# Transposes and sums of logarithms as two 64-row products, and a low-rank product spread over four column groups

## The chip, the core and the metric

The kernel runs on one core of one Trainium2 chip. A core has five engines that work side by side: TensorE (PE in the profile) for matrix products and transposes, with its weight loads shown apart (PEld); VectorE (DVE) and ScalarE (ACT) for elementwise work and for taking results out of PSUM; GpSimd (POOL); and SyncE (SP), whose queue issues the DMAs here. The metric is the device time of one execution in microseconds (us). A profile shows one execution; the span of its instructions is a little shorter than its time.

## The reference

Two blocks in a row. The first is a gated linear attention, a recurrence over 768 tokens for each of 4 batches and 8 heads of 48 channels; its output, with heads side by side, is the input of the second, a token mixer of rank 32 followed by a channel network of 384, 1536 and 384 channels.

```python
def _attn_ref(q, k, v, f_logit):            # (4, 8, 768, 48)
    f = 1.0 / (1.0 + np.exp(-f_logit))
    for t in range(S):
        state = f[:, :, t, :, None] * state + np.einsum('bhd,bhe->bhde', k[:, :, t], v[:, :, t])
        y[:, :, t] = np.einsum('bhd,bhde->bhe', q[:, :, t], state)

def _moe_ref(x, U, V, w_ch1, w_ch2):        # x: (4, 768, 384), U: (768, 32), V: (32, 768)
    h = x.transpose(0, 2, 1) @ U @ V
    u = x + h.transpose(0, 2, 1)
    return u + np.maximum(u @ w_ch1, 0.0) @ w_ch2
```

All data is float32 (the weights U, V, w_ch1 and w_ch2 arrive as float64 and are turned into float32 on the chip).

## The kernel before

**Attention.** The 768 tokens of a batch are cut into 6 blocks of 128 (NBL), each of two chunks of 64 (C). A unit is one batch and two heads, 96 channels padded to 128 partitions, so there are 16 units, four to a batch. Within a chunk the recurrence becomes matrix products, after q and k have been multiplied by running products of the gates. For that q, k and the gates are needed with channels on partitions and time along the row, while they arrive with time on partitions. How they are turned differs by unit:

- Units 0 to 3 (batch 0): `on_tensor` (L723) turns k and q with six TensorE transposes of 128x128 each, and VectorE multiplies the result straight out of PSUM (`operand`, L737). The running products of the gates come from sums of logarithms: `log_sums` (L764) multiplies each block of logarithms (128 tokens by 128 channels) by the constant matrix `later`, 128 x 130, which holds a 64x64 triangle for each chunk and, in two more columns, the sum over a whole chunk. `keep_logs` (L777 to L782) exponentiates the sums on ScalarE.
- Units 4 and 5: f, k and q through `on_tensor`, then a sigmoid on ScalarE (L788) and scans on VectorE.
- Units 6 to 15: turned by VectorE's own transpose (L700). TensorE isn't used for it.

A unit then goes through `kept` (L924, transposes of k by halves: 64 partitions to 128x64, two at a time), `scores` (L897), `states` (L945), a scan over chunks (L967), `read` (L984) and `inner` (L1002).

**Mixer.** One for each batch, on x with tokens on partitions, six blocks of 128 tokens by 384 channels. `low_rank` (L182) multiplies each token block by its 128x32 piece of U. An output of 32 rows uses 32 columns of the array, so four token blocks run beside each other in four column groups; blocks 4 and 5 follow in groups 0 and 1. `added_up` (L190) adds the four groups up with the constant matrix `blocks`, and `mix` (L207) multiplies by V. `turn` (L255) transposes the mixed x of two token blocks with six transposes of 128x128 into PSUM and ScalarE copies them to uT (L256); `ch1` (L267) and `ch2` (L327) or their versions with fewer products (L356, L454) are the channel network. Mixer 0 has finer pieces: `low_rank_of` (L218), `added_up_of` (L227), `mix_of` (L243), `turn_of` (L279, copy L281), `ch1_of` (L293); `low_rank_of` runs on 288 channels first and on 96 later, when the last unit of the batch is done.

**Order.** The order on TensorE is written out by hand over the whole kernel: the mixer of one batch runs between the pieces of the next batch's attention. VectorE, ScalarE and the DMA queue also have a written order in batch 0; later ScalarE and VectorE are ordered by the program's order with priorities. In batch 0 the chain of one unit on TensorE is: `log_sums` of the next unit (L764), scores (L897), k transposes of the next unit (L723), read (L984), q transposes of the next unit (L723), kept (L924), inner (L1002), states (L945), then `log_sums` of the unit after that, which waits for ScalarE's logarithms (L757, L758), which wait for VectorE's floor (L755), which stands behind the multiplication of q (L737) in VectorE's order.

**PSUM.** Wide results (two banks) take turns in three buffers (`ps_big`), narrow ones in two (`ps_mm`).

A matrix product in float32 stands in the profile as two records, a transpose as one.

Of the kernel before, what the change touches and what calls it, by code (L numbers as in the profile page):

```python
# [156 lines left out]
class Mixer:  # L157
# [6 lines left out]
    def __init__(self, tc, b, x, U, V, w1, w2, sums, ident, blocks, out, two, three, zp, ps_big, ps_mm, wide=False,  # L164
# [11 lines left out]

        def low_rank():
            pm = ps_mm.tile([P, 512], F32, name="ph", tag="mm")

            for c in range(NCH):  # L180
                g = slice((c % NG) * R, (c % NG + 1) * R)
                nc.tensor.matmul(pm[g, 0:DM], lhsT=U[:, c, :], rhs=x[:, c, :],  # L182
                                 start=(c < NG), stop=(c >= NCH - NG))
            h[0] = two.tile([P, DM], F32, name="h", bufs=2)
            nc.scalar.copy(h[0], pm[:, 0:DM])
# [28 lines left out]
        def low_rank_of(cols):  # L214
            pm = ps_mm.tile([P, 512], F32, name="ph", tag="mm")
            for c in range(NCH):
                g = slice((c % NG) * R, (c % NG + 1) * R)
                nc.tensor.matmul(pm[g, cols], lhsT=U[:, c, :], rhs=x[:, c, cols],  # L218
                                 start=(c < NG), stop=(c >= NCH - NG))
# [29 lines left out]
        def turn(a):  # L249
# [3 lines left out]
            for s in range(2):  # L253
                for m in range(NDC):
                    nc.tensor.transpose(pt[:, s, m * P : (m + 1) * P], x[:, 2 * a + s, m * P : (m + 1) * P], ident)  # L255
            nc.scalar.copy(  # L256
                uT[a].rearrange("p m (s t) -> p s m t", s=2),
                pt[:, :, 0 : NDC * P].rearrange("p s (m t) -> p s m t", t=P),
# [12 lines left out]
        def turn_of(a, ms):  # L271
# [4 lines left out]
            pt = last["put"]  # L276
            for m in ms:
                for s in range(2):
                    nc.tensor.transpose(pt[:, s, m * P : (m + 1) * P], x[:, 2 * a + s, m * P : (m + 1) * P], ident)  # L279
            g = slice(ms[0], ms[-1] + 1)  # L280
            nc.scalar.copy(  # L281
                uT[a][:, g].rearrange("p m (s t) -> p s m t", s=2),
                pt[:, :, ms[0] * P : (ms[-1] + 1) * P].rearrange("p s (m t) -> p s m t", t=P),
            )
# [232 lines left out]
def factored_path(ctx, tc, q, k, v, f_logit, moe_U, moe_V, moe_w_ch1, moe_w_ch2, out, ok):  # L517
# [108 lines left out]
    later = const.tile([P, P + 2], F32, name="later")  # L626
    nc.vector.memset(later, 0.0)
    for s in range(2):
        half = later[s * C : (s + 1) * C, s * C : (s + 1) * C]
        nc.vector.memset(half, 1.0)  # L630
        nc.vector.memset(later[s * C : (s + 1) * C, P + s : P + s + 1], 1.0)
# [74 lines left out]
    def prepare(n):  # L706
# [12 lines left out]
        def on_tensor(nm):  # L719

            pt = ps_big.tile([P, 2, 512], F32, name="pt", tag="big")
            for c in range(NBL):
                nc.tensor.transpose(  # L723
                    pt[:, 2 * c // NBL, c % (NBL // 2) * P : (c % (NBL // 2) + 1) * P],
                    nat[n % 2][nm][:, c].rearrange("p h d -> p (h d)"), ident,
                )
            return pt[:, :, 0 : G * C].rearrange("p a (c t) -> p a c t", t=C)

        def halves(t):
            return t[:, 0:S].rearrange("p (a c t) -> p a c t", a=2, t=C)  # L730

        def operand(nm, of):
            t = T[nm] = kz[n % 2][:, C:] if nm == "k" else two.tile([P, S], F32, name="qT")
            if n < HP:
                pt = on_tensor(nm).rearrange("p a c t -> p a (c t)").rearrange("p a (c t) -> p t a c", c=NBL // 2)
                by_time = "p (t a c) -> p t a c"
                nc.vector.tensor_tensor(t.rearrange(by_time, a=2, c=NBL // 2), pt,  # L737
                                        T[of].rearrange(by_time, a=2, c=NBL // 2), ALU.mult)
# [21 lines left out]
        def log_sums():  # L760
            pt = T["sums"] = ps_big.tile([P, 2, 512], F32, name="pt", tag="big")
            for c in range(NBL):
                o = c % (NBL // 2) * (P + 2)
                nc.tensor.matmul(  # L764
                    pt[:, 2 * c // NBL, o : o + P + 2],
                    lhsT=nat[n % 2]["f"][:, c].rearrange("p h d -> p (h d)"), rhs=later, start=True, stop=True,
                )
# [813 lines left out]
```

## Time and profile before

| | us |
|---|---|
| median of 3 runs | 477.74 (477.48 to 478.96) |
| the profiled execution | 477.89 |
| its span | 476.2 |
| granted TensorE clock over the span | 0.998 |

| Group (records) | busy us | shape |
|---|---|---|
| transposes L723 (84) | 11.6 | 128 rows to 128x128 |
| transposes L255 and L279 (72) | 9.2 | 128 rows to 128x128 |
| sums of logarithms L764 (48) | 6.6 | 128 rows, 128x130 |
| low rank L182 and L218 (60) | 6.2 | 128 rows, 32 columns of the array |
| half transposes L924 (192) | 9.4 | 64 rows to 128x64 |
| channel network L267, L293, L327, L356, L454 | 380 | 128 rows |

The busy time of a group is the time in which at least one of its records runs. Records overlap, so the mean length of a record (272 ns for a transpose) is longer than its step to the next (109 ns in a row of transposes). What a group costs TensorE is therefore read from start to start in the timeline, not from the lengths. TensorE is busy for most of every fortieth of the span; the table says how little of that the changed groups make up, about 34 us of 460.

### The profile page before, as it was taken

Reading aid. Unit: us, or ns where it says so; the run is one execution under the profiler, and the core shown is the slowest. Engines: PE = TensorE matmul, PEld = TensorE weight load, DVE = VectorE, ACT = ScalarE, POOL = GpSimd, SP = SyncE. Lnnn points to the kernel's source line nnn. Section 1 sums busy time; section 2 is a strip of 40 time slices with the busy share of each in tenths; the row PEclk is TensorE's granted clock in tenths of the full one; section 3 lists DMA queues with packets and bytes.
Section 4 is the critical chain, followed back from the end, with each engine's and each line's share of the span. In section 5 each row is a group of like instructions: output and inputs, shape, how many; then the busy total and the mean of one; then the engine's idle time right before and its main releaser. Section 6 shows DMA issues by size and latency. Waiting matters only on the chain.

```text
span 476.2 us, 12778 instructions
## 1 busy us (share of the span) xinstructions
PE 459.8 (97%) x5547; PEld 397.5 (83%) x5547; DVE 349.0 (73%) x579; ACT 179.1 (38%) x327; POOL 36.1 (8%) x48
## 2 busy tenths in 40 slices
PE   7998999999999899999999999999999999999995
PEld 5886888875665478798898888999979999999994
DVE  5768789789999485677766538987796887858632
ACT  5775876663443133414242423451411311212200
POOL 2002345441000000000000000000000000000000
PEclk9999999999999999999999999999999999999999
DMA  9948987577777322155416100100000000000001
GB/s 193 192 117 199 218 201 187 128 137 110 115 116 129 59 43 34 24 70 99 60 36 100 27 33 3 28 3 21 17 1 1 34 1 31 5 4 30 2 34 39
DMA packets 148312, 34.35 MB, mean 72 GB/s; under 512 B 136790, under 2 KB 146710, under 8 KB 148246
## 3 DMA queue, kind: packets, MB, share of 16 engines
q1 hardware_dynamic: 148246, 33.44, 35.6%
q8 instruction: 45, 0.74, 0.7%
q14 instruction: 21, 0.17, 0.1%
HBM read 28.70 MB, written 4.72 MB: 70 GB/s over the span
## 4 chain that ended last, share of the span: by engine, by line
PE 75%; DVE 13%; DMA 3%; issue 3%; ACT 3%; SPq 2%; POOL 0%; DVEq 0%
PE pw L356 26%; PE pz L267 22%; PE pp L454 12%; PE sc L897 2%; DVE late L819 2%; PE po L327 2%; PE y L984 2%; PE put L255 2%; PE y L1002 1%; DVE added L967 1%; PE pt L924 1%; DVE late L801 1%; PE pu L207 1%; PE pt L764 1%; SPq L600 1%
## 5 line engine op out<-in xcount | busy, mean ns | idle before, releaser
L267 PE MATMUL pz<-uT,w 128*128 128x256 f32 x492 | 111.4, 382 | 1.1 <-ACT z_all L310 1.1
L267 PEld LDWEIGHTS pz<-uT,w 128*128 128x128 f32 x492 | 91.7, 190 | 14.0 <-ACT z_all L310 1.5
L356 PE MATMUL pw<-w,z_all 128*128 128x192 f32 x216 | 37.7, 329 | 0.0
L356 PE MATMUL pw<-zw,w_raw 128*128 128x192 f32 x216 | 37.3, 327 | 0.0
L356 PEld LDWEIGHTS pw<-zw,w_raw 128*128 128x128 f32 x216 | 35.2, 190 | 0.7 <-DVE w_raw L197 0.6
L356 PEld LDWEIGHTS pw<-w,z_all 128*128 128x128 f32 x216 | 35.0, 190 | 0.7
L310 ACT ACTIVATE z_all<-pz 128x512 f32<-128x512 f32 x33 | 19.7, 598 | 41.8 <-PE pz L267 41.6
L101 POOL TENSOR_TENSOR w<-w_y,w_r 128x384 int32<-128x384 int32 x24 | 31.5, 1311 | 38.8 <-DVE w_y L100 23.5
L972 ACT COPY st<-added 128x576 f32<-128x576 f32 x12 | 14.7, 1223 | 39.0 <-DVE added L967 39.0
L454 PE MATMUL pp<-v_nat,late 128*128 128x128 f32 x224 | 28.8, 275 | 0.0
L454 PEld LDWEIGHTS pp<-v_nat,late 128*128 128x128 f32 x224 | 27.0, 192 | 0.0
L327 PE MATMUL po<-w,z_all 128*128 128x384 f32 x72 | 24.9, 493 | 1.6 <-DVE o L197 1.6
L447 ACT ACTIVATE other<-other 128x512 f32<-128x512 f32 x18 | 11.3, 631 | 39.9 <-DVE other L197 39.9
L327 PE MATMUL po<-w,zw 128*128 128x384 f32 x72 | 25.3, 496 | 0.1
L910 DVE TENSOR_TENSOR A<-sc,causal 128x768 f32<-128x768 f32 x16 | 15.2, 951 | 12.2 <-PE sc L897 11.9
L801 DVE TENSOR_TENSOR_SCAN late<-fz,late 128x768 f32<-128x768 f32 x12 | 21.1, 1755 | 4.0 <-ACT fz L796 3.6
L327 PEld LDWEIGHTS po<-w,z_all 128*128 128x128 f32 x72 | 13.3, 190 | 10.5 <-DVE o L197 2.3
L327 PEld LDWEIGHTS po<-w,zw 128*128 128x128 f32 x72 | 13.1, 190 | 9.8 <-issue 1.2
L819 DVE TENSOR_TENSOR_SCAN late<-fz,other 128x768 f32<-128x768 f32 x12 | 21.0, 1747 | 0.2
L447 ACT ACTIVATE z_all<-z_all 128x512 f32<-128x512 f32 x12 | 7.6, 630 | 32.8 <-DVE z_all L197 32.8
L984 PEld LDWEIGHTS y<-st,qT 48*64 48x64 f32 x704 | 13.5, 137 | 7.1 <-issue 4.5
L952 ACT COPY added<-ds 48x576 f32<-48x576 f32 (+1 forms) x28 | 17.8, 636 | 3.9 <-PE ds L945 3.7
(223 smaller groups left out, 848.1 us busy)
## 6 DMA issues: line engine op xcount, KB each, us to landing
w_raw<-in_moe_w_ch_dram SPq DMA_DIRECT2D x18, 384.0 KB, 3.5
out_dram<-o SPq DMA_DIRECT2D x24, 192.0 KB, 1.9
v_nat<-in_v_dram SPq DMA_DIRECT2D x16, 144.0 KB, 3.7
v_nat<-in_v_dram SPq DMA_DIRECT2D x32, 72.0 KB, 3.7
zw<-in_moe_w_ch_dram SPq DMA_DIRECT2D x6, 384.0 KB, 4.9
w<-in_k_dram SPq DMA_DIRECT2D x4, 288.0 KB, 5.0
w<-in_q_dram SPq DMA_DIRECT2D x4, 288.0 KB, 5.6
late<-in_f_logit_dram SPq DMA_DIRECT2D x10, 96.0 KB, 2.8
```

The lines of the kernel that those rows point to most:

```text
L101: nc.gpsimd.tensor_tensor(dst.bitcast(I32), shaped(y.bitcast(I32)), shaped(r), ALU.add)
L267: nc.tensor.matmul(pm[:, i * 2 * P : (i + 1) * 2 * P], lhsT=w1[:, m, o : o + P], rhs=uT[a][:, m, :], start=(m == 0), stop=(m == NDC - 1))
L310: nc.scalar.activation(z[a, c][:, k : k + 2, :].rearrange("p i t -> p (i t)"), pm, AF.Relu)
L327: nc.tensor.matmul(pm, lhsT=z[a, i // NI][:, i % NI, s * P : (s + 1) * P], rhs=w2[:, i, :], start=(i == 0), stop=(i == NFC - 1))
L356: nc.tensor.matmul(pm[:, n * HM : (n + 1) * HM], lhsT=lhs[:, i, :], rhs=rhs[:, i, :], start=(i == 0), stop=(i == NI - 1))
L447: nc.scalar.activation(dst, dst, AF.Relu, scale=float(SIGNS[n]))
L454: nc.tensor.matmul(pm[:, i, r * P : (r + 1) * P], lhsT=room["w"](wn)[:, r * P : (r + 1) * P], rhs=x_node(a, xn), start=((xn, wn) == of[0]) ...
L801: nc.vector.tensor_tensor_scan(backwards(X, S - 1, S), backwards(f, S, S), backwards(ends, S - 1, S), 0.0, ALU.mult, ALU.add,)
L819: nc.vector.tensor_tensor_scan(Y, f[:, 0:S], starts, 0.0, ALU.mult, ALU.add)
L910: nc.vector.tensor_tensor(T["A"], sc[:, :, 0 : NBL * C].rearrange("p h (c i) -> p h c i", i=C), causal.unsqueeze(1).unsqueeze(1).broadcast ...
L952: nc.scalar.copy(added[r, 1:].rearrange("p (e c s) -> p e c s", c=NBL, s=2), ds[r, :, 0 : NBL * D].rearrange("p s (c e) -> p e c s", e=D),)
L984: nc.tensor.matmul(o(c % 2, par, c // 2), lhsT=T["q"][rows[par], chunk[c]], rhs=T["st"][rows[par], c, :], start=(c <= 2), stop=False, skip ...
```

## The change

Four groups of TensorE products are cut in another way. What is computed stays the same.

- `on_tensor`: each 128x128 transpose becomes two transposes of 64 partitions (a chunk) by 128 columns, which use the upper and the lower half of the array's rows. Chunk s of every block goes to PSUM bank s. VectorE and ScalarE read with patterns changed to suit (L737, L740, L788, L789).
- `turn` and `turn_of`: the same, through a new helper `turn_blocks`, with the two halves in two banks and the copy to uT by runs of 64 instead of 128.
- `log_sums`: each product of 128 rows by 130 columns becomes two of 64 rows by 65 columns, also in the two halves of the rows. `later` shrinks to 128 x 65 and needs one fill instead of five.
- `low_rank` and `low_rank_of`: a new helper `products_with_u`. Token blocks 0 to 3 go to the four column groups as before. Blocks 4 and 5 are cut in two halves of the channels, and the four halves go to the four groups. `added_up` adds the groups up anyway.

On TensorE the order of the groups is unchanged. On the DMA queue one weight load of batch 1 (a piece of w_ch2) moves behind one load of q; on GpSimd the building of the identity matrix moves one step.

```diff
+        def products_with_u(pm, cols):
+            left = NCH - NG
+            n = (cols.stop - cols.start) * left // NG
+            todo = [(c, c, cols) for c in range(NG)]
+            todo += [(i % left + NG, i, slice(cols.start + i // left * n, cols.start + (i // left + 1) * n)) for i in range(NG)]
+            for c, i, of in todo:
+                nc.tensor.matmul(pm[i * R : (i + 1) * R, of], lhsT=U[:, c, :], rhs=x[:, c, of],
+                                 start=(c < NG), stop=True, skip_group_check=True)
...
-            for c in range(NCH):
-                g = slice((c % NG) * R, (c % NG + 1) * R)
-                nc.tensor.matmul(pm[g, 0:DM], lhsT=U[:, c, :], rhs=x[:, c, :],
-                                 start=(c < NG), stop=(c >= NCH - NG))
+            products_with_u(pm, slice(0, DM))
...
-            for s in range(2):
-                for m in range(NDC):
-                    nc.tensor.transpose(pt[:, s, m * P : (m + 1) * P], x[:, 2 * a + s, m * P : (m + 1) * P], ident)
+            turn_blocks(a, range(NDC), pt)
+
+        def turn_blocks(a, ms, pt):
+            H = P // 2
+            for m in ms:
+                for s in range(2):
+                    for r in range(2):
+                        g = slice(r * H, (r + 1) * H)
+                        o = (2 * m + s) * H
+                        nc.tensor.transpose(pt[:, r, o : o + H], x[g, 2 * a + s, m * P : (m + 1) * P], ident[g, g])
             nc.scalar.copy(
-                uT[a].rearrange("p m (s t) -> p s m t", s=2),
-                pt[:, :, 0 : NDC * P].rearrange("p s (m t) -> p s m t", t=P),
+                uT[a][:, ms[0] : ms[-1] + 1].rearrange("p m (s r t) -> p r (m s) t", s=2, r=2),
+                pt[:, :, 2 * ms[0] * H : 2 * (ms[-1] + 1) * H].rearrange("p r (n t) -> p r n t", t=H),
             )
...
-    later = const.tile([P, P + 2], F32, name="later")
-    nc.vector.memset(later, 0.0)
+    later = const.tile([P, C + 1], F32, name="later")
+    nc.vector.memset(later, 1.0)
...
             for c in range(NBL):
-                nc.tensor.transpose(
-                    pt[:, 2 * c // NBL, c % (NBL // 2) * P : (c % (NBL // 2) + 1) * P],
-                    nat[n % 2][nm][:, c].rearrange("p h d -> p (h d)"), ident,
-                )
+                for s in range(2):
+                    g = slice(s * C, (s + 1) * C)
+                    nc.tensor.transpose(
+                        pt[:, s, c * C : (c + 1) * C], nat[n % 2][nm][g, c].rearrange("p h d -> p (h d)"), ident[g, g],
+                    )
...
             for c in range(NBL):
-                o = c % (NBL // 2) * (P + 2)
-                nc.tensor.matmul(
-                    pt[:, 2 * c // NBL, o : o + P + 2],
-                    lhsT=nat[n % 2]["f"][:, c].rearrange("p h d -> p (h d)"), rhs=later, start=True, stop=True,
-                )
+                for s in range(2):
+                    g = slice(s * C, (s + 1) * C)
+                    nc.tensor.matmul(
+                        pt[:, s, c * (C + 1) : (c + 1) * (C + 1)],
+                        lhsT=nat[n % 2]["f"][g, c].rearrange("p h d -> p (h d)"), rhs=later[g, :], start=True, stop=True,
+                    )
```

## The prediction

> **What bounds the kernel now.** I read the page first, then the chain of waits in order of time, then the timeline around each changed group. Two lines of the page:
>
> ```profile
> PE 459.8 (97%) x5547; PEld 397.5 (83%) x5547; DVE 349.0 (73%) x579; ACT 179.1 (38%) x327; POOL 36.1 (8%) x48
> ...
> PE 75%; DVE 13%; DMA 3%; issue 3%; ACT 3%; SPq 2%; POOL 0%; DVEq 0%
> ```
>
> TensorE is busy for 97% of the span and makes three quarters of the chain that sets the end. VectorE holds 13% of it, and the chain in order of time puts that mostly at 104 to 160 us, and again around 336 to 352. A saving on TensorE therefore counts unless the next thing TensorE meets is a wait for another engine.
>
> The timeline gives the price of both forms, since `kept` (L924) already transposes by halves, and of the step between forms:
>
> ```profile
> 57.40 0.59 PE L267 MATMUL pz<-uT,w 128*128 128x256 f32 x2
> 57.84 0.82 PE L723 MATMUL pt<-ident,late 128*128 128x128 f32 x6
> 58.49 0.38 PE L267 MATMUL pz<-uT,w 128*128 128x256 f32 x1
> ...
> 96.54 0.81 PE L267 MATMUL pz<-uT,w 128*128 128x256 f32 x3
> 97.28 0.27 PE L897 MATMUL sc<-qT,kz 48*64 48x64 f32 x2
> ...
> 98.14 0.59 PE L924 MATMUL pt<-ident,kz 64*128 64x64 f32 x12
> 98.66 0.48 PE L267 MATMUL pz<-uT,w 128*128 128x256 f32 x1
> ...
> 45.03 0.53 PE L243 MATMUL pu<-h,V 32*128 32x96 f32 x6
> ```
>
> Columns: start, length of the whole group, engine, line, tiles, shape, records. From the first lines: two pz take 0.44 us from start to start, 0.22 each; six whole transposes take 0.65 (58.49 - 57.84), 109 ns each, and there is no gap at either side. From the next: three pz would be over at 96.54 + 3 x 0.216 = 97.19, but sc, in another shape of the array, starts at 97.28. Leaving the full shape costs 93 ns. From L924: twelve halves, which are six pairs, take 0.52 (98.66 - 98.14) from their first start to the first full product after them; single records in the trace split this into 110 ns for the first pair, 62 to 64 for each of four more, and 152 for the last pair and the way back. So n blocks by halves cost 93 + 110 + 63.5(n - 2) + 152 ns, whole 109n: 609 against 654 for six blocks, 1371 against 1962 for eighteen, but 355 against 218 for two. Short groups gain little or lose; the entry and the exit eat it.
>
> **The change part by part.** I sum over the places in order of time, with what waits behind each.
>
> *Batch 0, 0 to 34 us.* One loop of the chain runs from the sums of unit 3 (L764, 28.19) to the multiplication of its q (33.60). Its end:
>
> ```profile
> 31.47 1.23 PE L984 MATMUL y<-st,qT 48*64 48x48 f32 x44
> ...
> 32.63 0.87 PE L723 MATMUL pt<-ident,other 128*128 128x128 f32 x6
> ...
> 33.60 0.96 DVE L737 TENSOR_TENSOR qT<-pt,fz 128x768 f32<-128x768 f32 x1 [1.06 <-ACT seen L991]
> ```
>
> The k transposes (30.58) are not worth anything here: y needs a wide PSUM buffer, the sums' own, which ScalarE gives back when L779 ends, 31.23 + 0.19 = 31.42, and y starts at 31.47. The q transposes (32.63) are on the path: qT starts when their last record ends (the releaser named is long done by then), and the next unit's floor, logarithms and sums hang on qT in VectorE's order. Their last record ends 0.87 after the first start; by halves it is 110 + 4 x 63.5 + 222 (a record of L924) = 0.59, and the way in from y, 192 ns in the trace, should fall to about the 149 from sc to L924. Together 0.32 a loop, three loops (units 1, 2, 3): 0.96.
>
> The sums have no twin. Twelve records stand 112 ns apart after a first step of 215. By halves there are twelve pairs of records, each record moving 65 columns but loading 128 columns of weights. The nearest row is L243, 128-column weights in row tiles with 96 moving columns: its six records start within 0.53 - 0.27 (one record's length) = 0.26 us, two steps of 0.11 and 0.04 within a pair. So pairs do run side by side, and the load, not the moving side, paces them at 0.11: twelve steps, as before. What is left is 0.03 in the first step and 0.04 in a shorter last record, 0.07 for each of four units, 0.28, and I take that. Bounds: at best the pace of L924 (63 ns a pair), 10 x 0.048 = 0.5 more for each unit; at worst the two halves run one after the other, 24 records at 112, 1.2 us longer for each.
>
> The DMAs are early enough for this: k and q of unit 3 land at 25.5 and 26.7 and are unpacked at 26.6 and 27.0, with 1.8 us of idle VectorE before the scan behind them; f of unit 3 lands at 19.7 and is read at 26.25. If they were late after all, the 1.24 is lost (first rival). ScalarE's and VectorE's new patterns I cost at nothing: 576 elements in runs of 48 (L1008) take ScalarE 636 ns and 635 in long runs (L952), and VectorE takes 951 for 768 from PSUM in runs of 64 (L910) and 955 in L737. Four fills fewer on VectorE (0.34 us by its timeline) lie at 1.5 to 1.9 us, while it waits for f until 4.55: nothing.
>
> *34 to 46 us.* Low rank on 288 and 96 channels would save 0.24 and 0.08, and the four-block turn (L279) changes too, but each runs into a wait: y at 38.78 for VectorE's scan, put at 44.11 for VectorE's sum, pu at 44.87. Nothing either way.
>
> *46 to 100 us.* TensorE is busy without a break. The two-block turn costs 0.14 more, two six-block turns save 0.04 each, six groups of `on_tensor` (units 4 and 5) 0.04 each: -0.19 in all. Then, to 160, VectorE and DMA hold the chain; its start at about 92 hangs on what came before, so the sum so far, 1.43, is carried through. At 101.5 VectorE waits 0.2 for ScalarE and TensorE, so 0.08 of the last groups passes too.
>
> *Mixers 1 to 3, 152 to 376 us.*
>
> ```profile
> 267.23 1.49 PE L182 MATMUL ph<-x,U 128*32 128x384 f32 x12
> 268.65 0.43 PE L356 MATMUL pw<-zw,w_raw 128*128 128x192 f32 x1
> ...
> 281.31 2.13 PE L255 MATMUL put<-ident,x 128*128 128x128 f32 x18
> 283.28 0.38 PE L267 MATMUL pz<-uT,w 128*128 128x256 f32 x1
> ```
>
> Low rank takes 1.42 (268.65 - 267.23): four steps of 0.32 (hi and lo parts of blocks 0 to 3, then of 4 and 5), and 0.09 to leave. With blocks 4 and 5 on half the columns the last two steps halve: -0.32. At 267 it counts. At 152.7 it is swallowed by the wait that ends at 160.52, and at 342.2 by the one that ends at 351.66, both for VectorE (po in L327 is released by VectorE's o, pu in L207 by its x). So 0.32, not 0.96.
>
> The eighteen-block turn would save 0.59, but the first pz needs the first uT. Today ScalarE's copy starts when the sixth transpose is out (282.17) and takes 0.80; pz starts after it anyway. By halves, the sixth pair is out 0.09 + 0.36 + 0.22 after the old start, 0.04 later the copy begins, takes 0.80, and 0.05 on pz can start: 1.57 against 1.97. So 0.40, at 170 and at 281: 0.80, with ScalarE the one waited for. Mixer 3's turns come as six (359.3) and twelve (374.2): 0.04 and 1308 - 990 = 0.32, with other products behind them that don't wait for the copy. From 360 on TensorE has no gap to the end.
>
> Sum: 0.96 + 0.28 + 0.19 + 0.32 + 0.80 + 0.36 = 2.9 us. From the profiled execution's 477.89 that gives **475.0 us** (its time is 0.15 over the median, 477.74).
>
> [...]
>
> **Rivals.**
>
> - *The early gain is lost.* The DMA queue issues back to back from 0.8 to 25 us, and the landings become the clock of batch 0. For: the data of units 1 to 3 lands 0.7 to 2 us ahead of use in some places. Against: the copies that use it have idle VectorE behind them. Then 2.9 - 1.24 = 1.7 remain: 476.2.
> - *The halves of the sums run one after the other* (slower). Place: L764 in batch 0, four units, all on the chain. Price: 1.2 us each, 4.9, less the 2.6 that the rest brings: 477.9 + 2.3 = 480.2. It decides from about 170 ns a pair on (2.6 / 4 = 0.66 over twelve steps, on 112). For: no row here has 64-row tiles of full products with 128 columns. Against: L243 in 32-row tiles pairs them.
> - *The sums run at the pace of the half transposes.* 2.9 + 4 x 0.5 = 4.9: 473.0. For: the moving side is halved. Against: the load's pace in L243.
> - *The change of shape costs more in transposes than in scores*, or the two halves disturb each other at x or PSUM: 0.1 us on each of about 20 groups takes 2: 477.0.
>
> **How the numbers follow.** The sum as worked out 0.58, early gain lost 0.18, sums serial 0.08, sums faster 0.07, dearer shape 0.09. The likeliest alone spans 474.0 to 476.2. The range takes in the lost gain and the dearer shape above and reaches half way to the faster sums below, and leaves out the serial sums: 473.4 to 477.5. What a measurement of this kernel can tell from no change is about 0.3%, 1.4 us: faster means under 476.3. From the likeliest 0.57, the faster sums 0.07 and half of the lost gain 0.09: 0.73. Same: the other half 0.09 and the dearer shape 0.07: 0.16. Slower: 0.11.
>
> **What would show it.** Right: L723 and L255 with pairs 62 ns apart; L764 pairs 0.11 apart; qT of unit 3 near 32.4 instead of 33.60; the turn at 281 taking 1.57 with pz released by the uT copy; low rank 1.09 long; the waits before 160.5 and 351.7 longer by 0.3. Wrong: pairs at 110 ns in the transposes, sums longer than 1.6 us, qT's start unmoved, or a new TensorE gap in front of pz above 0.3.

## The result, and the profile after

The changed kernel is slower, not faster: 483.38 us (median of 14 runs, 479.66 to 487.61) beside 477.70 us for the kernel before (14 runs, 477.35 to 479.17). The ratio is 1.0108 (95% interval 1.0082 to 1.0133); it leaves out the two longest runs of the changed kernel, 486.93 and 487.61 us, which lie over 1.5% above its fastest. The prediction was 475.0. The changed kernel's runs lie 8 us apart, those of the kernel before 1.8. The profiled execution took 482.74 us, span 481.0.

Two lines of the page of the changed kernel, then two of its waits (what TensorE waited for: us in total, times, longest):

```profile
PE 462.5 (96%) x5771; PEld 398.3 (83%) x5771; DVE 349.0 (73%) x575; ACT 179.0 (37%) x327; POOL 36.1 (8%) x48
...
PE 77%; DVE 12%; ACT 3%; issue 3%; DMA 2%; SPq 1%; POOL 0%; DVEq 0%
```

```profile
PE ds L944 <- issue: 1.7, 4, 0.5
...
PE sc L896 <- issue: 1.3, 1, 1.3
```

TensorE has 224 more loads and 224 more products. It is busy for 2.7 us more although the halves should shorten it, and it has pauses in `ds` and `sc` in which it waits for nothing that the profile shows ("issue"). Of the four in `ds`, two (0.54 us at 123.3 and 0.33 us at 135.4) are old: they stand at the start of a group and in the kernel before as well, as `PE ds L945 <- issue: 0.9, 2, 0.6`. The other two and the one in `sc` are new.

The timeline shows a first cause. The sums of logarithms and the scores after them, of the changed kernel and then of the one before:

```profile
5.92 2.83 PE L767 MATMUL pt<-later,late 64*128 64x65 f32 x24 [0.33 <-issue]
...
15.53 2.82 PE L767 MATMUL pt<-later,other 64*128 64x65 f32 x24
...
24.48 1.56 PE L767 MATMUL pt<-later,late 64*128 64x65 f32 x24
25.97 0.93 PE L896 MATMUL sc<-qT,kz 48*64 48x64 f32 x48
```

```profile
5.91 1.81 PE L764 MATMUL pt<-later,late 128*128 128x130 f32 x12 [0.32 <-issue]
...
12.54 1.61 PE L764 MATMUL pt<-later,other 128*128 128x130 f32 x12
...
19.95 1.61 PE L764 MATMUL pt<-later,late 128*128 128x130 f32 x12 [0.59 <-ACT late L758]
21.49 0.93 PE L897 MATMUL sc<-qT,kz 48*64 48x64 f32 x48
```

For units 0 and 1 the sums take 2.83 us, for unit 2, the same work, 1.56. Up to 24.3 us the other groups that are as before are longer too (sc 1.56 instead of 0.93, y of L983 1.52 instead of 1.24). The trace's clock events say why: full clock is granted at 24.31 us, in the kernel before at 6.40. Before 24.31 the pairs of its sums start 213 ns apart, after it 112; and where the clock is taken away later in the run, at 478.28 us, the record says 0.5. Both are called half clock below. (The page's row of the granted clock shows 9s there all the same, as it has no event to go by before the first.) When sc of unit 2 starts, the changed kernel is 25.97 - 21.49 = 4.48 us late, nearly the whole loss of the profiled execution (482.74 - 477.89 = 4.85).

The second cause, two of the pauses, both in the middle of a group:

```profile
30.74 0.79 PE L944 MATMUL ds<-v_nat,kb 64*64 64x48 f32 x36
32.05 0.43 PE L944 MATMUL ds<-v_nat,kb 64*64 64x48 f32 x12 [0.52 <-issue]
...
321.61 0.79 PE L896 MATMUL sc<-qT,kz 48*64 48x64 f32 x35
323.69 0.45 PE L896 MATMUL sc<-qT,kz 48*64 48x64 f32 x12 [1.29 <-issue]
```

The remaining lines answer to those of the prediction: the end of unit 3's loop, single groups of six blocks between pz, low rank, and a turn of eighteen blocks. Two lines of the kernel before stand behind them, for the single groups.

```profile
36.83 0.59 PE L727 MATMUL pt<-ident,other 64*128 64x64 f32 x12
...
37.52 0.96 DVE L739 TENSOR_TENSOR qT<-pt,fz 128x768 f32<-128x768 f32 x1 [0.80 <-ACT seen L990]
...
62.22 0.58 PE L727 MATMUL pt<-ident,late 64*128 64x64 f32 x12
62.73 5.45 PE L279 MATMUL pz<-uT,w 128*128 128x256 f32 x24
68.11 0.58 PE L727 MATMUL pt<-ident,late 64*128 64x64 f32 x12
...
271.52 1.18 PE L184 MATMUL ph<-x,U 128*32 128x384 f32 x16
272.62 2.54 PE L360 MATMUL pw<-zw,w_raw 128*128 128x192 f32 x14
...
285.39 1.33 PE L267 MATMUL put<-ident,x 64*128 64x64 f32 x36
286.87 2.86 PE L279 MATMUL pz<-uT,w 128*128 128x256 f32 x12
```

```profile
58.49 5.35 PE L267 MATMUL pz<-uT,w 128*128 128x256 f32 x24
63.67 0.82 PE L723 MATMUL pt<-ident,late 128*128 128x128 f32 x6
```

Here the prediction holds or nearly holds: q follows the transposes' start after 0.69 us instead of 0.97, low rank takes 1.10 instead of 1.42, the turn 1.48 instead of 1.97. How far the same group stands behind its place in the kernel before tells where the time came and went:

| place in the kernel before, us | changed kernel later by, us | what lies between |
|---|---|---|
| 21.5 (sc of unit 2) | 4.48 | half clock up to 24.31 |
| 34.0 (y of unit 3) | 3.77 | two loops with half transposes at full clock, and the pause of 0.52 |
| 36.5 (low rank) | 4.33 | among others a pause of 0.31 in ds |
| 47.0 to 85.9 (pz) | 4.07 to 4.57 | single groups by halves |
| 172, 273, 283 | 4.19, 3.98, 3.59 | a turn, low rank, a turn |
| 318.8 | 5.30 | the pause of 1.29 |
| 375, 384 | 5.05, 5.15 | the last turns |

**What the pauses are.** The page's list of DMA queues has one of kind "instruction", here of the kernel before, then of the changed one, which has 448 more instructions of TensorE (packets, MB, share of 16 engines):

```profile
q8 instruction: 45, 0.74, 0.7%
```

```profile
q8 instruction: 47, 0.77, 0.7%
```

In the trace each of these packets has 16,384 bytes. If TensorE's instructions are numbered from 0 in the order in which the trace has them start, the pauses above stand before 1217 and 9153, and the third (0.31 us in ds at 39.83) before 1729. All three are 193 more than a multiple of 256, so that a packet would be 256 instructions of 64 bytes. The reading is that TensorE has used up a packet and the next isn't usable yet: packet n holds the instructions from 193 + 256n on. In the traces of all sixteen kernels of this study there are 33 pauses over 0.2 us in front of an instruction that waits for no semaphore. All 33 stand before such a number, and each ends 1.22 to 1.63 us after the packet has landed. No packet started before the instruction 320 ahead of its first one had been reached; from there its start took 0.9 us at best and in batch 0 up to 7. These traces have 692 such borders between packets, so 659 of them pass without a pause over 0.2 us. Where one doesn't, the pause costs 0.2 to 2.7 us.

### The profile page after: what moved, and what is told of

Read it like the earlier page. It is cut to its first block, busy times and chain, and to the rows that moved or that the text cites. A ratio compares the mean times of both kernels' runs of the same rounds, so it can differ in the third digit from the quotient of the medians.

```text
span 481.0 us, 13224 instructions
## 1 busy us (share of the span) xinstructions
PE 462.5 (96%) x5771; PEld 398.3 (83%) x5771; DVE 349.0 (73%) x575; ACT 179.0 (37%) x327; POOL 36.1 (8%) x48
## 4 chain that ended last, share of the span: by engine, by line
PE 77%; DVE 12%; ACT 3%; issue 3%; DMA 2%; SPq 1%; POOL 0%; DVEq 0%
PE pw L360 26%; PE pz L279 22%; PE pp L458 12%; PE y L983 2%; PE sc L896 2%; PE pt L767 2%; DVE late L818 2%; PE po L331 2%; PE y L1001 2%; PE ds L944 2%; DVE added L966 1%; PE pt L923 1%; PE idle L1092 1%; DMA other<-in_f_logit_dram 1%; DVE late L800 1%
## 5 line engine op out<-in xcount | busy, mean ns | idle before, releaser
L360 PEld LDWEIGHTS pw<-zw,w_raw 128*128 128x128 f32 x216 | 35.2, 190 | 0.4 <-DVE w_raw L204 0.3
L98 DVE TENSOR_SCALAR w_y<-w_y 128x384 f32<-128x384 f32 (+3 forms) x27 | 11.9, 440 | 10.4 <-ACT w_y L91 10.4
```

The lines of the kernel that those rows point to most:

```text
L360: nc.tensor.matmul(pm[:, n * HM : (n + 1) * HM], lhsT=lhs[:, i, :], rhs=rhs[:, i, :], start=(i == 0), stop=(i == NI - 1))
```

## The experiments

All runs in one table; "beside" is the median of the kernel before on the same chip, the two last columns are of the profiled execution. Clock: when full clock was granted, and when it was taken away. Pauses: number of the instruction, us.

| run | median (range; runs) | beside | ratio (95%) | clock | pauses |
|---|---|---|---|---|---|
| e1_sums_whole | 483.54 (481.99-486.12; 4) | 478.36 | 1.0117 (1.0051-1.0184) | 4.59; half 45.6-52.4 | 705 0.27, 961 0.34, 1729 0.95, 1985 2.54 |
| e2_sums_only | 486.12 (483.06-487.94; 4) | 478.36 | 1.0147 (1.0075-1.0218) | 13.54; half 34.0-44.3 | 705 0.28, 1217 0.95 |
| e3_no_warm | 479.19 (478.82-481.16; 10) | 478.36 | 1.0016 (0.9989-1.0043) | 9.43 | none |
| e4_66 | 483.83 (483.38-486.97; 4) | 478.36 | 1.0122 (1.0055-1.0188) | 5.38; half 15.6-29.3, 49.8-53.2 | 449 0.63, 1217 0.65, 9153 1.11 |
| e6_late_only | 478.63 (478.04-482.97; 12) | 478.05 | 1.0017 (0.9996-1.0039) | 6.44 | 8897 1.12 |
| e7_tiny | 485.15 (484.84-486.94; 4) | 478.05 | 1.0158 (1.0134-1.0182) | 4.62; half 45.6-55.8 | 705 0.57, 1985 2.70 |
| e8_wide | 483.69 (481.96-485.25; 4) | 478.05 | 1.0121 (1.0091-1.0150) | 4.29; half 45.3-52.1 | 1729 0.43, 1985 1.63 |
| e9_long_turns | 477.55 (476.34-480.56; 12) | 478.13 | 0.9989 (0.9968-1.0010) | 5.95 | 961 0.33 |
| e11_late_padded | 477.70 (476.80-479.49; 11) | 478.13 | 0.9987 (0.9975-1.0000) | 6.61 | 1217 0.78 |
| e10_q_too | 478.49 (476.94-480.69; 12) | 478.13 | 1.0017 (1.0000-1.0033) | 7.07; half 41.2-44.6 | 961 0.31, 1217 1.01 |
| e12_after_wide | 482.63 (480.97-488.08; 6) | 478.68 | 1.0105 (1.0067-1.0143) | 5.75; half 26.2-29.7 | 449 0.46, 705 1.31, 961 0.57, 1729 0.71, 9153 1.42 |
| e13_held_later | 479.55 (478.51-483.67; 12) | 478.44 | 1.0032 (1.0005-1.0059) | 6.57 | 705 0.57, 1985 0.22 |
| e14_whole_held | 479.08 (476.66-483.49; 12) | 478.00 | 1.0025 (0.9995-1.0055) | 5.47; half 39.6-53.3 | 961 0.46, 1217 0.36, 1729 2.20 |
| e15_long_held | 477.26 (476.68-478.12; 12) | 478.00 | 0.9976 (0.9958-0.9995) | 7.44 | 961 0.33, 1217 0.67 |

**Which part loses the time?** The first theory was the clock alone: the sums by halves feed the array too little to have full clock granted.

e1_sums_whole, the changed kernel with the sums as before:

```diff
-                for s in range(2):
-                    g = slice(s * C, (s + 1) * C)
-                    nc.tensor.matmul(pt[:, s, c * (C + 1) : (c + 1) * (C + 1)], lhsT=nat[n % 2]["f"][g, c]..., rhs=later[g, :], ...)
+                nc.tensor.matmul(pt[:, 2 * c // NBL, o : o + P + 2], lhsT=nat[n % 2]["f"][:, c]..., rhs=later, ...)
```

> The change without its sums: the logarithms are summed again in whole 128-row products with 130 columns, transposes and low rank stay as changed. Theory (the clock is granted late because of the sums by halves): the grant comes at about 6.4 us as in the kernel before, the sums of unit 0 take 1.8 us instead of 2.83, the runs lie within about 2 us of each other, and the time is 475.0 to 476.2, since the trace of the changed kernel shows that its loops of batch 0, its turns and its low rank do save about 2.3 us together once the clock is full. Rival (the half transposes keep the clock down as well): the grant comes after 10 us, 479 to 484 us with a wide scatter.

The clock came early, as the theory wants, at 4.59 (ahead of the first sums, at 6.12, so that the whole sums had no part in it), and the time didn't follow: 483.54. The timeline shows a pause of 2.54 us in the second low rank of batch 0:

```profile
42.19 0.27 PE L184 MATMUL ph<-x,U 128*32 128x96 f32 x1
45.00 0.45 PE L184 MATMUL ph<-x,U 128*32 128x96 f32 x15 [2.54 <-issue]
```

It stands before instruction 1985, and after it the clock was halved from 45.55 to 52.38. So the theory of the clock alone falls, and the rival with it, which wanted a late grant.

e2_sums_only, the kernel before with only the sums by halves (the same edit the other way round, with `later` of 65 columns):

> The kernel before with only the sums of logarithms by halves (pairs of 64 rows, 65 columns). Theory (late clock): the first full clock in the records comes well after 10 us, units 0 and 1 run at half speed, 481 to 486 us, with runs up to 6 us apart. Rival (the halves cost what they cost at full speed, 0.05 us less for each unit): 477.4 to 477.8 and a narrow scatter. Second rival (the extra 224 records, not the clock, bring pauses of TensorE's instruction stream): under 480, with pauses of 0.5 us or more without a releaser.

486.12: the sums alone, 48 products and 48 loads more (the 224 of the expectation are the whole change's), lose about as much as the whole change; the two intervals overlap. Both of the things expected by the theory and by the second rival are there: grant at 13.54, and pauses of 0.28 and 0.95 us, the second followed by ten us of half clock.

e3_no_warm, the kernel before without `busy(3)`:

```diff
-        busy(3)
```

> The kernel before without the three blank products ahead of the first sums; nothing else is changed (the blank products compute nothing that is used). Theory: the price of a late clock alone. TensorE's first work is then the whole sums at 5.9 us, the grant comes several us later than 6.4, units 0 and 1 run partly at half speed, and the time is 479 to 484 with a wide scatter. Rival (the clock's grant costs nothing, TensorE waits for other engines in batch 0 anyway): 477.3 to 478.2.

The grant comes at 9.43 instead of 6.40, and the kernel is 0.8 us slower, an interval that still holds no difference. Three us of half clock at that place cost 0.8 us by the medians, and between nothing and 2 us by the interval; no pause appears.

e4_66, the changed kernel with an even number of moved columns:

```diff
-    later = const.tile([P, C + 1], F32, name="later")
+    later = const.tile([P, C + 2], F32, name="later")
...
-                        pt[:, s, c * (C + 1) : (c + 1) * (C + 1)],
+                        pt[:, s, c * (C + 2) : (c + 1) * (C + 2)],
```

> The changed kernel with 66 instead of 65 columns moved in each product of the sums (one column of ones twice, its result isn't read). Theory A (the pair is paced by its two loads of 128 columns): steps of 112 ns at full clock as with 65, late grant, 480 to 487 us. Theory B (the odd number of columns, or results that begin at odd places, cost half the speed): steps of 62 to 70 ns, each unit's sums 0.5 us shorter at full clock, and the array streams for longer of the time, so that the grant may come early: 473.5 to 476 us; with the grant still late 477 to 483.

```profile
12.30 1.56 PE L767 MATMUL pt<-later,other 64*128 64x66 f32 x24
```

1.56 us at full clock, as with 65: theory A's time, not theory B's. That the two loads pace the pair isn't shown by this alone. This time the clock was granted at 5.38 and lost again from 15.62 to 29.27, in the middle of a pause of 0.63 us (15.38 to 16.01) at instruction 449, which follows a wait of 0.45. The time is that of the changed kernel by another path.

**Is it the instructions?** e7_tiny leaves all the work of the kernel before as it is and adds 52 pairs that take hardly any of the array's time:

```diff
+        def tiny(n):
+            for _ in range(n):
+                nc.tensor.matmul(idle[0:1, 0:8], lhsT=ident[:, 0:1], rhs=ident[:, 0:8], start=True, stop=True)
...
+            pieces += ([lambda: tiny(10)] if n == 0 else []) + rear(n, "kept")
...
+            for _ in range(8 if n > 1 else 0):
+                nc.tensor.matmul(pt[0:1, 0, 400:408], lhsT=ident[:, 0:1], rhs=ident[:, 0:8], start=True, stop=True)
```

> The kernel before with 52 more load and product pairs in batch 0 (one column loaded, eight moved, each about 30 ns), put where TensorE waits for ScalarE anyway: 20 ahead of the transposes by halves of unit 0, 16 each ahead of the sums of units 2 and 3; their results are not read. Theory (TensorE's instructions come in packets of 256, and the packets are late while the loads of batch 0 fill the DMA rings): a pause without a releaser at instruction 705, close to 20 us, perhaps more at 961, 1217 or 1729, each at 193 plus a multiple of 256, and 479 to 483 us. Rival (only the array's time counts, and these lie in waits): 477.5 to 478.3, no new pause.

485.15, 7 us lost to 1.7 us of small products that lay mostly in waits. The pause foretold at 705 is there (0.57 us), and at 1985 the one that e1_sums_whole has:

```profile
42.66 0.35 PE L218 MATMUL ph<-x,U 128*32 128x96 f32 x2
45.71 0.80 PE L218 MATMUL ph<-x,U 128*32 128x96 f32 x10 [2.70 <-issue]
```

Then ten us at half clock. So more instructions alone cost time, without any half product. In the profile of the kernel before, instruction 1985 runs at 48.76 and its packet has landed at 45.36; with some 100 instructions more in front of it it is due at 42.8.

e8_wide is e2_sums_only with twice the columns moved, so that the array is fed for a whole step:

```diff
-    later = const.tile([P, C + 1], F32, name="later")
+    later = const.tile([P, 2 * (C + 1)], F32, name="later")
...
-                        pt[:, s, c * (C + 1) : (c + 1) * (C + 1)],
+                        pt[:, s, c * (C + 1) : (c + 2) * (C + 1)],
```

> The kernel before with the sums by halves as in e2_sums_only, but each product moves 130 columns instead of 65 (65 more columns of ones, whose results the next block overwrites or nobody reads): as many instructions, the same loads, steps near 112 ns, and the array fed for nearly all of a step instead of half of it. Theory (the clock's grant follows how much of the time columns are moved): full clock at about 5 to 8 us and no fall during the sums, 479 to 483, with the pauses of e2_sums_only at instructions 705 and 1217 still there. Rival (the clock follows the pauses or the rows of a product, not the moved columns): grant after 10 us, 483 to 488 as in e2_sums_only.

```profile
12.36 1.61 PE L766 MATMUL pt<-later,other 64*128 64x130 f32 x24
```

Full clock at 4.29, none lost during the sums, and the group hardly longer than with 65 columns at full clock (1.56). But the first sums start at 5.83, after the grant, so this run doesn't tell whether the moved columns bring the clock. The time is 2.4 us less than in e2_sums_only by the medians of four runs each, whose ranges overlap, and 0.7 above what the theory said; the pauses did not stay at 705 and 1217 but stand at 1729 and 1985.

e12_after_wide does the same to the changed kernel:

```diff
-    later = const.tile([P, C + 1], F32, name="later")
+    later = const.tile([P, 2 * (C + 1)], F32, name="later")
```

> The changed kernel with 130 instead of 65 columns moved in each product of its sums by halves, the added ones' results overwritten or not read: same instructions, same loads, the array fed for twice the time. It takes the late clock out of the changed kernel and leaves its count of instructions. Theory (both causes count): full clock by about 8 us, and at full speed TensorE uses its instructions up faster, so pauses at instructions such as 705, 961, 1217, 1729 or 1985 take the place of the slow stretch: 480 to 484 us. Rival A (the late clock alone was the loss): 475 to 476.5, no pause beyond 0.3 us. Rival B (only the pauses count): 483 to 487 as before, with the grant as late as it was.

482.63 with full clock at 5.75, as the first sums start (5.73): the ratio, 1.0105, is that of the changed kernel (1.0108), so hardly any of the loss comes back with the clock. Five pauses, 4.5 us in all, take the place of the slow stretch, as the theory says. Rival A falls; rival B falls by its grant.

**The parts after batch 0.** e6_late_only keeps batch 0 as before and has by halves only units 4 and 5 and the turns of six blocks, and low rank split in batches 1 to 3:

```diff
+            if n >= HP:
+                for c in range(NBL):
+                    for s in range(2):
...
+            if len(ms) == NDC:
+                turn_blocks(a, ms, pt)
```

> The change without its batch 0: sums, transposes and low rank of batch 0 as before; by halves only the turns of six blocks and the transposes of units 4 and 5, and low rank of batches 1 to 3 split. Theory (the loss sits in the first 50 us, where TensorE runs out of fetched instructions and the clock falls; the later parts save what the trace of the changed kernel shows: 0.3 at low rank, 0.3 to 0.5 at each of two turns, 0.3 at the end): no pause without a releaser before 50 us, full clock from 6 to 8 us on, 475.8 to 476.8; with one pause near 320 us, where y, ds and sc follow each other closely, up to 478. Rival (the later parts cost something that the shift of the records hides): 477.5 or more without any pause.

478.63, no pause before 300 us, and a single one later:

```profile
317.39 0.48 PE L925 MATMUL sc<-qT,kz 48*64 48x64 f32 x17
319.00 0.69 PE L925 MATMUL sc<-qT,kz 48*64 48x64 f32 x30 [1.12 <-issue]
```

The kernel is 0.62 us ahead of the one before at 283 us and 0.85 behind at 319. That is 0.6 above what was expected even with such a pause: between 46 and 86 us the single groups lose 0.4.

e11_late_padded adds 50 small pairs to it in `added_up`, where mixer 1 waits anyway:

```diff
+            for _ in range(25 if b == 1 else 0):
+                nc.tensor.matmul(pm[0:1, 400:408], lhsT=ident[:, 0:1], rhs=ident[:, 0:8], start=True, stop=True)
```

> The kernel of e6_late_only with 50 more load and product pairs (one column loaded, eight moved, 32 ns each, results not read) in mixer 1, where TensorE waits 1.9 us for VectorE near 161 us. They do nothing but move the count of instructions by 100: instruction 8897 then lies 218 instructions into the dense stretch near 315 us instead of 318, and its packet is asked for about 5 us ahead instead of 2.6. Theory (packets of 256 instructions): the pause of 1.12 us at 318 is gone, and the kernel with more work is 0.9 to 1.2 us faster than e6_late_only, 477.2 to 477.7 beside its 478.6. Rival (the pause belongs to the place in the program, or to the transfers there): the pause stays, 478.6 or more.

```profile
160.58 1.40 PE L201 MATMUL ph<-ident 128*1 128x8 f32 x50 [0.57 <-ACT h L199]
...
318.47 0.92 PE L927 MATMUL sc<-qT,kz 48*64 48x64 f32 x47
319.31 2.22 PE L376 MATMUL pw<-w,z_all 128*128 128x192 f32 x12
```

The pause is gone, and the kernel with 1.4 us more work is 0.9 us faster, as foretold. In its profiled execution there is a pause of 0.78 us at 1217, in batch 0, which is that of the kernel before to the instruction. So the kernel before stands near this edge itself, and some of its own runs, up to 482.9 us in these jobs, may have gone over it; their traces were not taken.

e9_long_turns keeps of the change only what e6_late_only showed to pay:

```diff
+            if b in (1, 2) or (b == 3 and a):
+                turn_blocks(a, range(NDC), pt)
+                return
...
+            if b == 2:
+                products_with_u(pm, slice(0, DM))
```

> Only what the run of e6_late_only showed to pay: by halves the turns of 18 blocks in mixers 1 and 2 and of 12 in mixer 3, low rank split in mixer 2; everything else as before, all single groups of six blocks whole again. Theory (a lone group of six by halves costs 0.05 to 0.1 us more, a turn of 18 saves 0.39, low rank 0.32, the 12 blocks 0.2; and the dense stretch near 315 us begins 80 instructions later in the count than before, so that its packets end 166 and 422 instructions into it, both asked for early enough): no pause, 0.39 + 0.39 + 0.32 + 0.2 = 1.3 us under the kernel before, 476.2 to 476.8 where that has 477.7. Rival (the shift of the count puts a late packet into the dense stretch again): a pause of about 1 us near 320 and 477.4 to 478.

No pause near 320. The median, 477.55, lies above the range; the profiled execution took 476.84, with a pause of 0.33 us in batch 0, in code that was not touched. Whether longer ones there lift the other runs (476.34 to 480.56) isn't shown. At 384 us the kernel is 0.94 ahead, and it was 0.12 behind at 36 us: 1.06 gained by the later parts, where 1.3 was expected.

**Can the packets be had in time?** e10_q_too adds to that the transposes of q in units 1 to 3 (36 instructions in batch 0) and the 50 pairs of e11_late_padded.

```diff
+            if nm == "q" and 0 < n < HP:
+                for c in range(NBL):
+                    for s in range(2):
```

> e9_long_turns with the transposes of q of units 1 to 3 by halves as well (36 instructions more in batch 0) and the 50 small pairs in mixer 1 (100 instructions, hidden in the wait near 161 us), so that the packets of the dense stretch end 30 and 286 instructions into it. Theory: q's multiplication comes 0.3 us earlier in each of up to three loops, and instruction 1985 is reached only 36 instructions earlier than before, about when its packet can be used (46 us), so that at most a short pause stands there: 475.4 to 476.2. Rival (batch 0 has no room for 36 more instructions): a pause of 0.5 to 2.7 us at instruction 1985 and half clock after it, 477.5 to 482.

478.49. No pause at 1985, as the theory says, but one of 1.01 us at 1217, and the clock halved from 41.2 to 44.6. The time is the rival's, the place isn't. As e9_long_turns and e11_late_padded have shorter pauses at 961 and 1217 with batch 0 untouched, this run doesn't tell whether the 36 instructions brought it.

e13_held_later takes e7_tiny and moves the release of the next loads:

```diff
-                pieces += halves[1:2] + join[1:2] + rear(n - 1, "inner") + [held] + halves[2:]
+                pieces += halves[1:2] + join[1:2] + rear(n - 1, "inner") + halves[2:]
...
+        low_rank_of(done)
+        held()
         for load_w in weights[early + FIRST : early + FIRST + 4]:
```

> The kernel of e7_tiny (52 more small pairs in batch 0) with ScalarE's two small copies that release the next loads of weights and of units 4 and 5 put behind its copy of low rank's first result, so that these loads begin near 39 us instead of 36.3. Nothing else is changed. Theory (the packet that ends at instruction 1985 is asked for near 36.1 us and waits behind those loads until 42.9): it now starts by about 38.5 us and lands before 40, the pause of 2.7 us near 43 and the half clock after it are gone or under 0.5 us, and the time falls from 485 to between 479 and 482 although the loads come later. Rival (the lateness of that packet has nothing to do with these loads): the packet still starts after 41 us, pause of 2 us or more, 485 or more.

```profile
43.15 0.35 PE L218 MATMUL ph<-x,U 128*32 128x96 f32 x2
43.72 0.49 PE L218 MATMUL ph<-x,U 128*32 128x96 f32 x10 [0.22 <-issue]
```

485.15 becomes 479.55, the pause 0.22 instead of 2.70, and the clock stays. The loads begin at 39.46 instead of 36.30, and the packet of 1985 starts at 40.57 instead of 42.87. So the place of the loads matters to the packet here. But it starts two us later than the theory had it, 4.0 us after instruction 1665, although the core's DMA engines moved next to nothing from 36 to 40 us (busy share 0.02 and 0.00): the loads aren't all that holds it up, and what else does stays open. The same move was then made in e9_long_turns:

> e9_long_turns (only the long turns by halves and one low rank split) with the loads of weights and of units 4 and 5 released behind low rank's first copy, as in e13_held_later. Theory: the packet of instruction 1985 lands several us earlier, which this kernel of few instructions in batch 0 hardly needs, so the time is that of e9_long_turns or a little less, 476.3 to 477.5 and under the kernel before. Rival (the later loads make mixer 0 wait): 478 or more.

477.26, ratio 0.9976 (0.9958 to 0.9995): of all kernels here the only one whose interval lies below the kernel before, by 0.7 us. Its runs are also the closest together. The mechanism of the theory isn't seen, though: the packet of 1985 starts at 45.31, 6.98 us after instruction 1665, where e9_long_turns has 43.12 and 6.01. The loads are late, the packet isn't earlier, and the 0.3 us between the two medians is within their scatter. And in e1_sums_whole, by the same edit:

> e1_sums_whole (the whole change except that the sums are whole products again) with the same later release of the loads. Theory (the late packets were what lost the gain): no pause above 0.5 us at instruction 1985 and no half clock after it, the shorter pauses at 705, 961 and 1729 stay, 476 to 479 us instead of 483.5. Rival (the halves themselves cost what was lost): 481 or more.

The median falls from 483.54 to 479.08, above the range by a little. The runs are spread over 476.66 to 483.49: four of twelve took 476.7 to 477.4, inside the prediction's range, with a granted clock of 0.998 or 0.999, and four took 482 and more, with 0.980 to 0.985, among them the profiled one. That one has no pause at 1985, as the theory says, but 2.20 us at instruction 1729 and then half clock; the packet of 1729 started 2.7 us after instruction 1409, while the DMA engines moved nothing (busy share 0.00 from 32.5 to 35.2). So half transposes, turns and the split low rank can run without the loss. That the good runs have their packets in time fits, but their traces were not taken.

## Why the prediction was wrong

Taken step by step, what it says of TensorE's array mostly holds, and what it leaves out decides.

*Sums of logarithms.* Right on the chosen value: the pairs start 112 ns apart, and the group takes 1.49 us from start to start instead of 1.54, 0.05 where 0.07 was said. Neither the faster nor the serial halves came. That the loads set this pace was the author's estimate, from L243; the moved columns hardly do (the group is 1.56 us long with 65 and 66, 1.61 with 130, e8_wide). What failed is the step from there to the time: "twelve steps, as before" was taken to mean that nothing else changes. The clock didn't stay: full clock came at 24.31 in the changed kernel and at 13.54 in e2_sums_only. The cause of that is shown only in part. The stretches between two clock events are all multiples of 3.41 us (3.41 to 40.96). Counted back from the grant in such steps (an estimate from these stretches, no trace shows where a step begins), the step that ends at 7.24 in the changed kernel holds the end of the blank products and 1.3 us of sums by halves, and brought no grant; those that end at 7.07 in e10_q_too and at 7.44 in e15_long_held hold 1.1 and 1.6 us of whole sums in their place, and did. That speaks against the halves, in one profile each. With 66 and 130 columns (e4_66, e8_wide, e12_after_wide) the grant came at 5.38, 4.29 and 5.75, before the first sums or as they started, so that whether the moved columns decide it is not shown. Nor is it the sums alone: the step from 10.66 to 14.07 of the changed kernel has none, and brought no grant either.

*q in batch 0.* Right: 0.28 from the transposes to q, and the loop from unit 2 to unit 3 takes 7.93 us instead of 8.23, 0.30 where 0.32 + 0.07 was said. It can't be cashed in here, since the loops now contain pauses.

*46 to 100 us.* Wrong sign, -0.19 said, +0.5 measured. The formula's way into the half shape, 93 ns, was read from one place, three pz ahead of sc. A row of 24 pz ahead of six half blocks takes 68.11 - 62.73 = 5.38 us, ahead of six whole ones 63.67 - 58.49 = 5.18: 0.20, not 0.09. With that, six blocks by halves cost 0.05 more than whole instead of 0.045 less.

*Low rank and turns.* Right: 1.10 for 1.09 (the four steps are in the trace the first and second records of blocks 0 to 3, then of 4 and 5; what tells the two records of a product apart isn't shown), swallowed at 152.7 by a wait that is now 1.93 instead of 1.64, and at 342.2 by a new wait of 0.45 for VectorE's qT (the one before pu stayed at 0.55); the turn of 18 saves 0.38 and 0.39 for 0.40, with pz released by the copy of uT as foretold. Mixer 3 brings 0.16 instead of 0.36, the same 0.10 missing at each group.

*The sum.* The step that failed is not a term but a cost that no term holds. Every part was costed as array time, "so many blocks by so many ns", and the count of records was read from the page (x5547) without a price. By halves each block is twice as many instructions. What the runs showed in its place: 52 small pairs, 1.7 us of work that lay mostly in waits, cost 7 us (e7_tiny), and the changed kernel with its clock restored has 4.5 us of pauses at the borders of packets (e12_after_wide). The paragraph on early DMAs looks at k, q and f and finds them 0.7 to 2 us ahead; the packets of instructions come by DMA as well. In the kernel before, that of number 1985 landed at 45.36 and was usable by 46.99 at the latest (1.63 us on), some 23 instructions before TensorE needed it at 48.76. None of the rivals has this mechanism, so the range ended at 477.5. The page had a hint of it, the queue of kind "instruction" beside DMA engines at eight tenths or more in five of the first six slices, but no pause: that profile has none over 0.2 us at a border.

*How the loss divides* is settled only roughly. In the changed kernel's profile the half clock comes first, and with TensorE slower only three pauses over 0.2 us follow; take it away (e12_after_wide) and pauses cost nearly the same. The two can't be added. That a pause brings the clock down is likely but not shown: seven of nine falls in the middle of these traces have a pause within the 3.4 us before them, but 26 of the 33 pauses, of up to 1.42 us, have no fall behind them. Of the other two falls, one followed a wait of 1.29 us for VectorE, and one nothing longer than 0.29 us.

## What to carry to other kernels

Where a change turns few large products into many small ones, count its instructions next to its time: for each packet, take the time from the instruction 320 ahead of it to its first one, less the pause itself if there is one. In these sixteen traces 12 of 37 borders with under 5 us paused, 21 of 165 with 5 to 8 us, and none of the 490 with more. Short groups between full-shape products lose on the change of shape what a long run of small ones gains (0.05 us lost by six blocks between pz, 0.38 and 0.39 saved by a turn of 18), so only the long runs should be changed. A pause in the middle of a group that waits for nothing is a reason to number the instructions before looking for a cause in the code.

## What the runs showed of the hardware

- By the places of the pauses TensorE starts with 449 instructions (by the trace's count) and gets 256 with each packet; where it paused for one, it went on 1.22 to 1.63 us after the packet had landed. A kernel with 50 more products (e11_late_padded) was 0.9 us faster than e6_late_only: with the packets' borders moved, the pause of 1.12 us was gone.
- TensorE can be busy by the page without the clock being granted: in the changed kernel it worked from 1.38 to 10.03 us with one gap of 0.33, and full clock came at 24.31. Each stretch between two clock events here is a multiple of 3.41 us (3.41, 6.83, 10.24, 13.65, 20.48, 34.13, 40.96). A busy one of that length isn't enough for the grant, if the steps are counted back from it: the one from 3.83 to 7.24 was busy but for that gap, and brought none.
- Two loads of 128 columns side by side take 112 ns in the sums whether 65, 66 or 130 columns are moved, and 62 ns in transposes of the same shape (both at full clock). Why these differ was not tried.
